# Second layer of a convolution + feed-forward kernel: a fourth product by a second level of Strassen, one unit fewer, and the jobs around it moved

## The chip, the cores and the metric

The kernel runs on one core of one Trainium2 chip. A core has five engines, each with its own in-order queue: TensorE (PE in the profile; its weight loads are PEld), VectorE (DVE), ScalarE (ACT), GpSimd (POOL) and SyncE (SP, which here only issues DMAs). They meet by semaphores. SBUF is the on-chip memory, PSUM the memory that TensorE writes (eight banks of 128 x 512 floats, used here as four slots of two banks). Transfers run on 16 DMA engines that all queues share; GpSimd's queue is q0 in the profile, SyncE's q1. The metric is the device time of one execution in microseconds.

## What is computed

```python
# x: (8, 4096, 192), weight: (8 heads, 7), w_in: (192, 2048), w_out: (2048, 192)
w = softmax(weight, axis=-1)                      # 7 taps per head
y[b, s, c] = sum_k w[c // 24, k] * x_pad[b, s + k, c]     # causal, 6 zeros ahead
h = y.reshape(32768, 192) @ w_in
g = h * np.clip(h + 3.0, 0.0, 6.0) / 6.0
out = g @ w_out                                   # (32768, 192)
```

All in float32.

## The kernel before

The tokens go in 32 blocks of 1024, each as two groups of 512 (the token halves). Block 0 runs by a plain path at start-up (`out_direct`, L379). Blocks 1 to 31 run `first_layer` (L498) and then `second_layer` (L586), and while one block is in these, VectorE and ScalarE prepare y of the next one.

**Convolution.** `conv_jobs` (L990) makes seven jobs: one ScalarE multiplication (L992) and six VectorE taps (L994) that each read x and y and write y (128 x 1536). They are hung into the stream of the other work by hand: `jobs` of the first layer (L1047: after step n of 16) and `between` of the second (L1058, L1060: at a unit of its clock). y is split into a high part (ScalarE, L476), a low one (VectorE, L1011) and a mixed one (L479), so that the first layer can run in TensorE's fast float32r form; `swap_parts` (L492) then issues six DMAs from GpSimd's queue that copy the three parts with their partition halves exchanged into `y_other`. `y_other` lies in the same memory as `z2` of the second layer.

**First layer.** 16 steps n. Each is 18 matmuls in three groups of six: HIGH and LOW (`begin`, L517), then MIX (`end`, L530). Between them the PSUM result is scaled (L522 on ScalarE; for n = 15 one half on ScalarE, L525, and one on VectorE, L526). After MIX come `relu` on ScalarE (L302) and the gate on VectorE (L306), which writes g and frees the step's PSUM slot; with four slots, step n + 2 begins in the slot of step n - 2. Steps 0 to 7 use y's own parts, steps 8 to 15 `y_other`. In TensorE's order a first layer has 48 groups of six; the last five are HIGH and LOW of n = 15 and MIX of n = 13, 14 and 15.

**Sums for the second layer.** g has four quarters A11, A21, A12, A22 (`g4`, L274): half of the 2048 hidden units by token half. The second layer multiplies them with w_out by Strassen's seven products P1 to P7 (`prod`, L417), of sums such as S1 = A21 + A22 (made in A21's place by DMAs with addition, L556), S2 = S1 - A11 (L414, `g_sums`), S3 = A11 - A21 (L414, in `s3`) and S4 = A12 - S2 (made in `s3` by L678 on ScalarE and adding DMAs, L679). Each product has three column groups q of 32. For P1, P2 and P5 the groups 0 and 1 are computed by Strassen once more, on halves of tokens and of the hidden units; this needs four smaller sums each (`small_sums`, L564; line L575): P1's by GpSimd during the first layer, in pairs of slots, into `shared`; P2's by VectorE into `z2`; P5's by VectorE into A22's place. Their weight sums `w_s` are made once (`small_weights`, L577).

**Second layer.** TensorE runs four streams side by side, each 32 columns wide, which write different partition quarters. The streams' order is written out by hand: `plain` (L621) is eight matmuls of 512 tokens at two units each, or some of them; `small` (L637) is one small product of four matmuls of 256 tokens at one unit each. All matmuls have one line, L616. `put` counts each stream's clock; `do(t, job)` hangs a job of another engine in at unit t; at the end all are sorted by unit and emitted in that order (L846), so each engine's queue has the order of these numbers. A product in plain form costs 16 units a column group, so 32 for two; by Strassen it costs 28. Before, all streams end at unit 81. Partial results are handed on inside PSUM by small ScalarE copies (L613, L750 to L755); `fold` (L673) adds up a second-level product on VectorE; the results are added (L458), transposed (L464) and stored by SyncE (L374), 128 bytes to a packet. `finish` (L801) does the last two of a block's four stores at the start of the next first layer.

PSUM slots: the second layer's banks `d, e, b, x_, a, c` (L589) lie in the slots of steps 12, 13 and 14, in this order by twos, and `f, h` in that of step 15. S1, as GpSimd's queue has it in the first layer: the pairs' sums for P1 (after n = 1, 3, 5, 7), then S3's first pair (after n = 9), a DMA into S1, S3's second pair (after n = 11), its DMA, and two more DMAs behind S3's last pairs, which VectorE makes (after n = 13 and 15).

Of the kernel before, what the change touches and what calls it, by code (L numbers as in the profile page):

```python
# [8 lines left out]
ALU = mybir.AluOpType  # L9
# [16 lines left out]
def kernel(  # L26
# [93 lines left out]
    w_s = cst.tile([P, 3, 4, NP // 2, QS], F32, name="w_s")  # L120
# [240 lines left out]
    def new_results():  # L361
        results[:] = [shared]
        xts[:] = 4, 5, 7
# [126 lines left out]
    y_own, y_other, pools = [], [None], []  # L490

    def swap_parts(dma=nc.sync):  # L492
        y_other[0] = pools[0].tile([P, 3, K3, N], F32, name="y_other", tag="other")
        for n in range(3):
            swap(y_other[0][:, n], y_own[n], dma)


    def first_layer(i, jobs):  # L498
# [44 lines left out]
        for n in range(count):  # L543
            if n == count - 3:
                begin(n + 2)
            end(n)
            if n < count - 3:
                begin(n + 2)
            for job in jobs.get(n, ()):
                job()  # L550
            if n < NP and n % 2:
                small_sums(shared, A11, (1, 2, 3, 4), nc.gpsimd, every[n - 1 : n + 1])
            if n > NP and n % 2:
                pair = slice(n - NP - 1, n - NP + 1)
                g_sums(nc.gpsimd if n + 3 < count else nc.vector, (3,), range(NP)[pair], 2)
                nc.gpsimd.dma_start(out=S1[:, pair], in_=A22[:, pair], accum_op=ALU.add)  # L556
# [20 lines left out]
    def small_weights(to, w):  # L577

        b11, b12, b21, b22 = (
            w_out[:, c::2, w, q * QS : (q + 1) * QS] for c in range(2) for q in range(2)  # L580
        )
        t1, t2, t3, t4 = (to[:, n] for n in range(4))
        for o, p, q in ((t1, b12, b11), (t2, b22, t1), (t3, b22, b12), (t4, b21, t2)):
            nc.gpsimd.tensor_tensor(out=o, in0=p, in1=q, op=ALU.subtract)

    def second_layer(i, between):  # L586
        last = i + 1 == NB
        ours = [free_slots.pop(0) for _ in range(3)]
        d, e, b, x_, a, c = (psum[:, 2 * n + k] for n in ours for k in range(2))  # L589
        z = pools[0].tile([P, NP + 1, N], F32, name="z2", tag="other")  # L590
# [10 lines left out]
        A, E, B, C = (bank[fourth, t] for bank in (e, x_) for t in halves)  # L601
        A2, E2, C2, B2 = f[first, lo], f[second, hi], h[first, lo], h[second, hi]
# [34 lines left out]
        def small(n, m_, out, start=False, j=3):  # L637
# [3 lines left out]
                1: (shared, w_s[:, 0]), 5: (s5, w_s[:, 1]), 2: (sums2, w_s[:, 2]),  # L641
            }[n]
            x11, x12, x21, x22 = four_parts(x)
            z1, z2, z3, z4 = four_parts(sums)
            b11, b12, b21, b22 = (
                w_out[:, h::2, w, q * QS : (q + 1) * QS] for h in range(2) for q in range(2)
            )
            t1, t2, t3, t4 = (ws[:, k] for k in range(4))
# [44 lines left out]

        plain(0, d, 4, 0, every, True)
        small(2, 1, A2, True, 0)
        after(0, copy, out=B2, in_=A2)
        plain(0, c, 7, 0, every[:3], True)
        by_half(0, a, 2, 2, 2, 1)
        after(0, copy, out=a[fourth], in_=a[first])
        plain(0, c, 7, 0, every[3:])  # L700
        small(2, 7, C2, False, 0)
        after(0, lambda: copy(out=p2(second, hi), in_=C2))
        small(2, 2, A2, False, 0)
        after(0, lambda: copy(out=p2(first, lo), in_=A2))
        plain(0, b, 6, 0, every)
        small(2, 4, C2, False, 0)
        p3(0)

        plain(1, d, 4, 1, every, True)
        plain(1, a, 2, 2, every[:2], True)  # L710
        by_half(1, a, 2, 2, 2, 0)
        after(1, copy, out=a[first], in_=a[second])
        plain(1, c, 7, 1, every[:2], True)
        small(2, 6, B2, False, 1)
        after(1, copy, out=C2, in_=B2)
        plain(1, c, 7, 1, every[2:])
        small(2, 5, E2, True, 1)
        after(1, lambda: copy(out=p2(second, lo), in_=E2))
        plain(1, b, 6, 1, every)
        small(2, 3, B2, False, 1)  # L720
        p3(1)

        plain(2, d, 4, 2, every[:6], True)
        plain(2, b, 1, 2, every[2:])
        after(2, copy, out=p1[third], in_=b[third])
        plain(2, c, 7, 2, every, True)
        plain(2, d, 4, 2, every[6:])
        by_half(2, a, 2, 2, 5, 1)
        plain(2, b, 6, 2, every)
        plain(2, a, 2, 2, every[6:])  # L730
        p3(2)

        def level_two(n, p, chunks, order):
            chunks, first_fill = list(chunks), [True]
            left = [list(chunks) for _ in halves]

            def fill_half(t, k):
                for _ in range(k):
                    ch = left[t].pop(0)
                    x, w = prod[n]  # L740
                    put(3, 1, lambda ch=ch: matmul(
                        3, (a, c)[t][fourth, halves[t]], w_out[:, ch, w, 2 * QS : 3 * QS],
                        x[:, ch, halves[t]], ch == 0,
                    ))

            def fill(k):
                plain(3, b, n, 2, [chunks.pop(0) for _ in range(k)], first_fill.pop() if first_fill else False)

# [6 lines left out]
                3: lambda: (copy(out=p()[first, hi], in_=C), fold(p(), B)),  # L755
            }
            to = {1: A, 2: A, 6: B, 5: E, 7: C, 3: B, 4: C}
            for step in order.split():
                if step[0] == "x":
                    fill(int(step[1]))  # L760
                elif step[0] in "lh":
                    fill_half("lh".index(step[0]), int(step[1]))
                else:
                    k = int(step)
                    small(n, k, to[k], k in (1, 5))
                    if k != 4:
                        do(clock[3], steps[k])

        level_two(1, lambda: p1, (), "1")
        plain(3, b, 1, 2, every[:2], True)  # L770
        after(3, copy, out=b[third], in_=V)
        level_two(1, lambda: p1, (), "6 2 7 5 4 3")
        plain(3, a, 2, 2, every[3:5])
        by_half(3, a, 2, 2, 5, 0)
        after(3, copy, out=a[third], in_=a[fourth])
        level_two(
            5, lambda: late["p5"], range(NP),
            "1 l8 6 2 7 5 4 3 h8" if last else "1 x6 6 2 7 5 4 3 x2",
        )
# [3 lines left out]
        do(0, small_sums, sums2, A12, (1, 2, 3, 4), nc.vector)  # L783
        do(33, tiles)
        do(28.5, g_sums, nc.vector, (2,), every[:4], 4)
        do(33, g_sums, nc.vector, (2,), every[4:], 4)
        do(35, copy, out=b[m], in_=p1)
        do(45, small_sums, s5, S1, (1, 2, 3, 4), nc.vector)
        for n, t in zip(range(0, NP, 2), (34, 39, 42, 45)):
            do(t, negative, slice(n, n + 2))  # L790
        do(41.2, lambda: copy(out=late["p7"], in_=c[m]))
        do(61.2, lambda: add(late["u3"], b[m], late["p7"]))
        do(62, lambda: add(late["p7"], late["u3"], d[m]))
        do(62, lambda: store(i, late["p7"], 1, 0))
# [79 lines left out]
    with tc.manual_schedule():  # L874
# [131 lines left out]
        def split_high():  # L1006
            high_of(y_own[HIGH][:], y[:])
# [87 lines left out]
```

## Time and profile before

| | |
|---|---|
| median of 3 runs (lowest, highest) | 2214.92 us (2214.84, 2214.95) |
| the profiled execution's own time | 2214.33 us |
| its span, first to last instruction | 2212.6 us |
| TensorE clock granted | 1.0 |
| busy: PE, PEld, DVE | 2205.5, 1619.9, 1888.4 us |
| busy: ACT, POOL | 1613.6, 1070.3 us |
| DMA: GpSimd's queue q0, SyncE's q1 | 47.8%, 14.6% of 16 engines' span |
| taps L994: 186, mean | 1.804 us |
| gates L306 of 128 x 1024: 496, mean | 1.218 us |
| GpSimd L414, 128 x 1024: 62, mean | 3.377 us |
| VectorE L575 of 128 x 1024: 124, mean | 1.222 us |
| adding DMA into S1 (512 KB), issue to landing | 5.7 us |
| swap of y (384 KB), issue to landing | 8.7 us |

The profile page gives the busy time of each engine, the chain of work that ended last (followed back from the last instruction), and the costliest groups: line, engine, operation, output <- input, shape and count, busy time and the mean of one, and the idle time of the engine ahead of them with whoever ended it. The timeline gives the same in order of time: start, length, engine and line, and in brackets the idle time before. All matmuls are pipelined, so that a busy PE need not be a PE at its peak, and a wait is put down to what came last. A share of busy time is an average over both layers; the stages have different limits.

### The profile page before, as it was taken

The page shows a single profiled execution, that of the slowest core. Times are in us where ns is not written, and L with a number is a line of the kernel's source. Part 1 is how long each engine was busy: PE and PEld are TensorE (multiplying, and loading weights), DVE is VectorE, ACT ScalarE, POOL GpSimd, SP SyncE. Part 2 cuts the span into 40 slices and gives each one's busy share as a digit, 9 for nine tenths or more (in the row PEclk, how much of TensorE's full clock was granted, in tenths as well). Part 3 has the DMA queues.
Part 4 walks back from the last instruction along what each step waited for, and adds up shares of the span by engine and source line. Part 5 has one row for each costly group of instructions (what it writes and reads, how often), then busy time and mean ns, then how long its engine had stood idle before and what let it go on. Part 6 is the DMA issues. An engine that isn't in the chain of part 4 may idle for free.

```text
span 2212.6 us, 53012 instructions
## 1 busy us (share of the span) xinstructions
PE 2205.5 (100%) x22364; PEld 1619.9 (73%) x22364; DVE 1888.4 (85%) x1766; ACT 1613.6 (73%) x2112; POOL 1070.3 (48%) x1029
## 2 busy tenths in 40 slices
PE   9999999999999999999999999999999999999999
PEld 5477777778777878777777777877777787777876
DVE  8888888888888888888888888888888888888876
ACT  7478776687766777767877668776677776687765
POOL 2455544455544555445554345554355544555533
PEclk9999999999999999999999999999999999999999
DMA  6265657656577656675565766666755667656575
GB/s 157 55 117 113 130 106 148 118 109 124 115 131 136 105 110 129 116 149 103 113 127 110 142 122 110 119 120 125 141 102 112 131 111 148 110 112 129 98 134 91
DMA packets 304190, 264.28 MB, mean 119 GB/s; under 512 B 210992, under 2 KB 216112, under 8 KB 303952
## 3 DMA queue, kind: packets, MB, share of 16 engines
q0 software_dynamic: 82240, 201.95, 47.8%
q1 hardware_dynamic: 220472, 58.67, 14.6%
q8 instruction: 175, 2.87, 0.6%
q14 instruction: 63, 0.52, 0.1%
q10 hardware_dynamic: 1240, 0.27, 0.1%
HBM read 31.72 MB, written 25.17 MB: 26 GB/s over the span
## 4 chain that ended last, share of the span: by engine, by line
PE 99%; DVE 0%; DMA 0%; SPq 0%; ACT 0%; issue 0%; DVEq 0%; ACTq 0%
PE psum L616 49%; PE psum L510 46%; PE psum L296 2%; PE psum L341 2%; DMA x<-in_x_dram 0%; DVE shared L458 0%; DVE shared L464 0%; SPq L100 0%; SPq L133 0%; DVE top L175 0%; PE psum L889 0%; DVE y L255 0%; SPq L89 0%; ACT y L903 0%; ACT scale L186 0%
## 5 line engine op out<-in xcount | busy, mean ns | idle before, releaser
L616 PE MATMUL psum<-g,w_out 128*32 128x512 f32 (+1 forms) x6340 | 899.5, 525 | 0.0
L306 DVE SCALAR_TENSOR_TENSOR g<-g,psum 128x1024 f32<-128x1024 f32 (+1 forms) x528 | 620.9, 1186 | 186.1 <-ACT g L302 185.7
L302 ACT ACTIVATE g<-psum,half 128x1024 f32<-128x1024 f32 (+1 forms) x528 | 564.9, 1087 | 6.0 <-PE psum L510 5.2
L616 PEld LDWEIGHTS psum<-g,w_out 128*32 128x32 f32 x6340 | 389.6, 110 | 217.6 <-issue 102.7
L510 PE MATMUL psum<-y,w_in 64*128 64x512 f32 x4464 | 522.2, 388 | 0.0
L510 PE MATMUL psum<-y_other,w_in 64*128 64x512 f32 x4464 | 516.6, 386 | 0.0
L522 ACT ACTIVATE psum<-psum 128x1024 f32<-128x1024 f32 x465 | 469.0, 1009 | 51.1 <-PE psum L510 48.8
L616 PE MATMUL psum<-s,w_out 128*32 128x512 f32 (+1 forms) x3024 | 503.7, 585 | 0.0
L510 PEld LDWEIGHTS psum<-y,w_in 64*128 64x128 f32 x4464 | 429.0, 184 | 100.8 <-issue 26.0
L510 PEld LDWEIGHTS psum<-y_other,w_in 64*128 64x128 f32 x4464 | 438.9, 184 | 67.0
L575 POOL TENSOR_TENSOR shared<-g 128x256 f32<-128x256 f32 x248 | 273.9, 1105 | 301.9 <-DVE g L306 301.9
L994 DVE SCALAR_TENSOR_TENSOR y<-x,c_sb,y 128x1536 f32<-128x1536 f32 x186 | 335.5, 1804 | 2.6 <-ACT y L992 1.4
L679 POOL DMA_DIRECT2D s<-g x124 | 148.5, 1202 | 341.1 <-ACT s L678 303.7
L616 PE MATMUL psum<-g,w_s 128*32 128x256 f32 x1488 | 285.5, 379 | 0.0
L556 POOL DMA_DIRECT2D g<-g x124 | 150.0, 1210 | 149.3 <-issue 76.8
L414 POOL TENSOR_TENSOR s<-g 128x1024 f32<-128x1024 f32 x62 | 209.4, 3377 | 24.8 <-DVE g L306 24.7
L616 PEld LDWEIGHTS psum<-s,w_out 128*32 128x32 f32 x3024 | 156.2, 110 | 53.3 <-issue 32.9
L616 PEld LDWEIGHTS psum<-g,w_s 128*32 128x32 f32 x1488 | 159.2, 110 | 42.6
L613 ACT COPY psum<-psum 32x512 f32<-32x512 f32 x186 | 89.4, 481 | 116.5 <-PE psum L616 113.4
L616 PE MATMUL psum<-shared,w_s 128*32 128x256 f32 x744 | 170.7, 379 | 0.0
L616 PE MATMUL psum<-z,w_s 128*32 128x256 f32 x744 | 170.6, 379 | 0.0
L575 DVE TENSOR_TENSOR g<-g 128x1024 f32<-128x1024 f32 x124 | 146.4, 1222 | 17.6 <-PE psum L616 14.4
(111 smaller groups left out, 2182.3 us busy)
## 6 DMA issues: line engine op xcount, KB each, us to landing
y_other<-y POOLq DMA_DIRECT2D x180, 384.0 KB, 8.7
g<-g POOLq DMA_DIRECT2D x124, 512.0 KB, 5.7
s<-g POOLq DMA_DIRECT2D x124, 512.0 KB, 6.6
out_dram<-shared SPq DMA_DIRECT2D x378, 64.0 KB, 4.0
x<-in_x_dram SPq DMA_DIRECT2D x53, 388.5 KB, 5.8
stage<-in_moe_w_in_dram SPq DMA_DIRECT2D x16, 192.0 KB, 4.4
stage<-in_moe_w_out_dram SPq DMA_DIRECT2D x8, 384.0 KB, 5.6
x<-in_x_dram SPq DMA_DIRECT2D x7, 384.0 KB, 4.6
```

The lines of the kernel that those rows point to most:

```text
L296: nc.tensor.matmul(out=psum[:, b], lhsT=w[r], rhs=src, start=start, stop=stop, skip_group_check=onto,)
L302: nc.scalar.activation(r6, h, ACT.Relu, bias=half[:], scale=1.0 / 6.0)
L306: nc.vector.scalar_tensor_tensor(out=g_, in0=g_, scalar=1.0, in1=h, op0=ALU.min, op1=ALU.mult)
L414: engine.tensor_tensor(out=o[:, r], in0=a[:, r], in1=b[:, r], op=op)
L510: nc.tensor.matmul(out=psum[:, 2 * slots[n] + k], lhsT=r32(w_in_parts[part][r, c, s]), rhs=r32(y_other[0][r, part, s] if group else y_own[ ...
L522: nc.scalar.mul(both(n), both(n), 4097.0)
L556: nc.gpsimd.dma_start(out=S1[:, pair], in_=A22[:, pair], accum_op=ALU.add)
L575: engine.tensor_tensor(out=o, in0=p, in1=q, op=op)
L613: streams[3].append((t - 0.5, lambda: fn(*args, **kw)))
L616: nc.tensor.matmul(out=out, lhsT=w, rhs=x, start=start, stop=True, tile_position=(0, j * QS), skip_group_check=True,)
L679: nc.gpsimd.dma_start(out=S3[:, pair], in_=A12[:, pair], accum_op=ALU.add)
L994: jobs.append(lambda k=k: nc.vector.scalar_tensor_tensor(out=y[:], in0=x[:, :, k : k + N], scalar=c_sb[:, k : k + 1], in1=y[:], op0=ALU.mu ...
```

## The change

- P4 = A22 x T4, columns 0 and 1, also by Strassen once more. Its four sums go into a new tile `z4`, which shares its memory with y's three own parts (pool `later`, tag `own`): GpSimd makes the first after n = 8 and the third after n = 9, VectorE the second after n = 14 and the fourth at the head of the second layer. Its results go to free places in `shared` (slots 4 and 5).
- The streams are written anew for 80 units: stream 0 begins with P4's third column group in bank b, stream 1 with P1's third column group in b, streams 2 and 3 with the first small products of P4 and P1. S1 times T1 (P5) is begun by stream 3 at unit 4. The bank letters `x_` and `a` change places.
- S3's third and fourth pair are both made after n = 15, by VectorE.
- y's parts come later in the second layer, since their memory holds `z4` before: high at 37, low at 62, mix at 63 (before: 9, 20, 46).
- One convolution tap a block is done as a multiplication on GpSimd into `s3` and an adding DMA onto y from GpSimd's queue, issued at the head of the next first layer, behind the six swaps; four taps follow on VectorE after n = 5, 7, 9 and 11, and one at unit 24 of the second layer. Before, VectorE did two taps at the end of the second layer, one at the head of the first and three after n = 1, 5 and 9.
- The weights' small sums are kept for four products; the third of each takes the place of a block of w_out that is no longer used.

The core of the diff:

```diff
-    w_s = cst.tile([P, 3, 4, NP // 2, QS], F32, name="w_s")
+    w_s = cst.tile([P, 4, 3, NP // 2, QS], F32, name="w_s")
...
-        xts[:] = 4, 5, 7
+        xts[:] = 7, 4, 5
...
-            if n > NP and n % 2:
-                pair = slice(n - NP - 1, n - NP + 1)
-                g_sums(nc.gpsimd if n + 3 < count else nc.vector, (3,), range(NP)[pair], 2)
-                nc.gpsimd.dma_start(out=S1[:, pair], in_=A22[:, pair], accum_op=ALU.add)
+            if n == NP:
+                sums4[:] = [pools[0].tile([P, NP, N], F32, name="z4", tag="own")]
+                small_sums(sums4[0], A22, (1,), nc.gpsimd)
+            if n in (NP + 1, NP + 3, count - 1):
+                for p in ((n - NP - 1) // 2,) if n < count - 1 else (2, 3):
+                    pair = slice(2 * p, 2 * p + 2)
+                    g_sums(nc.gpsimd if p < 2 else nc.vector, (3,), range(NP)[pair], 2)
+                    nc.gpsimd.dma_start(out=S1[:, pair], in_=A22[:, pair], accum_op=ALU.add)
+            if n == NP + 1:
+                small_sums(sums4[0], A22, (3,), nc.gpsimd)
+            if n == count - 2:
+                small_sums(sums4[0], A22, (2,), nc.vector)
...
-        d, e, b, x_, a, c = (psum[:, 2 * n + k] for n in ours for k in range(2))
+        d, e, b, a, x_, c = (psum[:, 2 * n + k] for n in ours for k in range(2))
...
-        plain(0, d, 4, 0, every, True)
+        plain(0, b, 4, 2, every, True)
         small(2, 1, A2, True, 0)
...
-        plain(1, d, 4, 1, every, True)
...
+        plain(1, b, 1, 2, every, True)
...
-        plain(2, d, 4, 2, every[:6], True)
...
+        level_two(4, lambda: p4, (1,), 2)
+        plain(2, c, 7, 2, every[:2], True)
+        level_two(4, lambda: p4, rest, 2)
+        plain(2, c, 7, 2, every[2:])
...
+        level_two(1, lambda: p1, (1,))
+        fill_half(0, 4) if last else fill(2)
+        level_two(1, lambda: p1, rest)
+        level_two(5, lambda: late["p5"], (1,))
+        plain(3, a, 2, 2, every[2:6])
+        fill_half(0, 4) if last else fill(4)
+        level_two(5, lambda: late["p5"], rest)
+        fill_half(1, 8) if last else fill(2)
+        assert clock == [80] * 4
...
-        do(0, small_sums, sums2, A12, (1, 2, 3, 4), nc.vector)
-        do(33, tiles)
+        do(0, small_sums, sums2, A12, (1, 2), nc.vector)
+        do(0, small_sums, sums4[0], A22, (4,), nc.vector)
+        do(0, small_sums, sums2, A12, (3,), nc.vector)
         do(28.5, g_sums, nc.vector, (2,), every[:4], 4)
+        do(32, tiles)
+        do(32, fold_with, p1)
         do(33, g_sums, nc.vector, (2,), every[4:], 4)
...
-        do(45, small_sums, s5, S1, (1, 2, 3, 4), nc.vector)
+        do(36, small_sums, s5, S1, (1, 2, 3, 4), nc.vector)
+        do(37, small_sums, sums2, A12, (4,), nc.vector)
+        do(38, fold_with, p4, 2)
...
+        def tap_by_dma(x, k):
+            to = S3[:, 0:K3]
+            nc.gpsimd.tensor_scalar(
+                out=to, in0=x[:, :, k : k + N], scalar1=c_sb[:, k : k + 1], scalar2=None,
+                op0=ALU.mult,
+            )
+            nc.gpsimd.dma_start(out=y[:], in_=to, accum_op=ALU.add)
...
-            jobs = {4 * n + 1: [job] for n, job in enumerate(conv[4:])}
-            jobs[-1] = left + conv[3:4]
+            jobs = {3 + 2 * n: [tap] for n, tap in enumerate(taps[:5]) if n}
+            k = KC - len(taps)
+            jobs[-1] = [lambda: tap_by_dma(conv_x[0], k)] * bool(taps) + left
...
-                between = [(9, split_high), (20, split_low), (46, split_mix), (70, lambda: swap_parts(nc.gpsimd))]
+                between += [(37, split_high), (62, split_low), (63, split_mix)]
+                between += [
+                    (t, lambda n=n: swap_parts(nc.gpsimd, (n,)))
+                    for n, t in ((HIGH, 70), (LOW, 70), (MIX, 70))
+                ]
...
-                between += [(20, begin_conv), (60, lambda: conv[0]()), (72, lambda: conv[1]()), (73, lambda: conv[2]())]
+                between += [(30, begin_conv), (74, lambda: conv[0]())]
```

## The prediction, made before the changed kernel had run

> **What bounds the kernel now.** I read the page first, then the chain that ended last, then one block on each engine in the timeline (block 14: first layer from 983.41 to 1016.32 us, second layer to 1051.36), then the DMA issues. The page gives TensorE the whole span, and so does the chain:
>
> ```profile
> span 2212.6 us, 53012 instructions
> PE 2205.5 (100%) x22364; PEld 1619.9 (73%) x22364; DVE 1888.4 (85%) x1766; ACT 1613.6 (73%) x2112; POOL 1070.3 (48%) x1029
> PE 99%; DVE 0%; DMA 0%; SPq 0%; ACT 0%; issue 0%; DVEq 0%; ACTq 0%
> ```
>
> The chain in order of time is a strict alternation, 32.9 us of first layer and 35.04 us of second layer:
>
> ```profile
> 847.54 32.95 PE psum L510 x286
> 880.49 35.04 PE psum L616 x256
> 915.53 32.91 PE psum L510 x288
> 948.44 35.04 PE psum L616 x255
> ```
>
> The same numbers come back for all 31 blocks, and inside a first layer six matmuls always take 0.68 us. So TensorE never waits: whatever it saves counts in full, and whatever it is made to wait counts in full. In the second layer one unit is 0.43 us (matmuls of one stream start 0.43 apart; 81 units are 34.8 of the 35.04).
>
> VectorE around the end of the first layer (start, length, line, idle before and who ended it):
>
> ```profile
> 1008.07 1.81 DVE L994 SCALAR_TENSOR_TENSOR y<-x,c_sb,y 128x1536 f32<-128x1536 f32 x1
> 1009.80 2.44 DVE L306 SCALAR_TENSOR_TENSOR g<-g,psum 128x1024 f32<-128x1024 f32 x2
> 1013.05 1.22 DVE L306 SCALAR_TENSOR_TENSOR g<-g,psum 128x1024 f32<-128x1024 f32 x1 [0.81 <-ACT g L302]
> 1014.41 0.70 DVE L526 TENSOR_SCALAR psum<-psum 128x512 f32<-128x512 f32 x1
> 1016.28 1.22 DVE L306 SCALAR_TENSOR_TENSOR g<-g,psum 128x1024 f32<-128x1024 f32 x1 [1.16 <-ACT g L302]
> ```
>
> The gate that starts at 1016.28 is that of n = 13. It waits for its relu, which waits for TensorE, so it ends at 1017.50 and cannot end earlier: 1.18 us after TensorE entered the second layer. GpSimd in the same first layer:
>
> ```profile
> 1000.08 2.25 POOL L575 TENSOR_TENSOR shared<-g 128x256 f32<-128x256 f32 x1 [0.74 <-DVE g L306]
> 1002.40 0.74 POOL L575 TENSOR_TENSOR shared<-shared,g 128x256 f32<-128x256 f32 x1
> ...
> 1008.23 3.92 POOL L414 TENSOR_TENSOR s<-g 128x1024 f32<-128x1024 f32 x1 [0.79 <-DVE g L306]
> 1012.46 1.24 POOL L556 DMA_DIRECT2D g<-g  x1 [0.30 <-POOL s L414]
> ```
>
> One 128x256 sum takes 0.74 us beside gates (which read PSUM) but 2.25 beside a convolution tap (L994, two SBUF inputs, 999.91 to 1001.72): it ends 0.61 after the tap. The 3.92 ends 2.27 after the tap that began at 1008.07. So the two do not overlap. Start-up shows the other direction: a tap that begins while GpSimd works takes 2.01 instead of 1.81, and ends 1.62 after GpSimd's op (102.78).
>
> ```profile
> 102.39 2.01 DVE L994 SCALAR_TENSOR_TENSOR y<-x,c_sb,y 128x1536 f32<-128x1536 f32 x1
> 101.72 1.06 POOL L584 TENSOR_TENSOR w_s<-w_out,w_s 128x128 f32<-128x128 f32 x1
> ```
>
> **The change, part by part**, against the profiled execution's own 2214.33 us (the median of the runs is 2214.92, 0.6 more).
>
> *One unit less.* P4's columns 0 and 1 cost 28 units instead of 32, over four streams: 81 to 80. Gain 0.43 us a block, 31 blocks: 13.3 us.
>
> *P4 comes first, in bank b.* The built program's first second-layer matmul now waits for gate 13, since b lies in that gate's PSUM slot. Before, stream 3 asked for this gate at unit 4 (1.72 us in, when it was done) and bank d needed only gate 12. Price: 1017.50 − 1016.32 = 1.2 us in every block. Nothing hides it, TensorE's queue is in order. It alone is 37 us, more than the gain.
>
> *P5 starts at unit 4.* Stream 3 now fills with P5 (S1) at unit 4; the program waits there for the first adding DMA into S1, and stream 2 beside it for the first pair of S3. Before, S1 was first asked for at unit 37, 15.9 us in; the DMA (issued 1012.46, landing 5.1 to 6.0 later) was done by then by far. This decides the forecast, so I lay out GpSimd's queue. It gets, ahead of S3's first pair (its 128x1024 difference), another 128x1024 sum (z4's first). The taps move to n = 5, 7, 9, 11. With the rule "one at a time, by turns" from the rows above:
> - Tap 5 at 999.91 as now; the four sums of the third pair, begun beside it, end at 1004.53 as now.
> - Gate 7 ends 1004.07 (its relu sets that). Tap 7 begins at 1003.99, is held to 1004.53 and ends 1.62 later: 1006.15.
> - The last pair's sums need gate 7 and are held to 1006.15; the first ends 0.6 later, three more by 0.70: 1008.9.
> - Gates 8 and 9 end 1008.4; tap 9 is held to 1008.9, ends 1010.5. z4's sum is held to that and takes 2.28: 1012.8.
> - Gates 10 and 11 end 1012.8; tap 11 ends 1014.45. S3's first pair: 1016.75.
> - 0.3 to the DMA's issue, 5.3 to its landing (rows 5.1 to 6.0): 1022.35.
>
> TensorE would reach unit 4 at 1016.32 + 1.72 = 1018.04: it waits 4.3 us, call it 4.4 with the wake-up. The 1.2 for gate 13 lies inside that.
>
> By the Trainium skill ("SBUF — State Buffer", section "Who interferes with whom") a VectorE instruction with two SBUF inputs and a GpSimd instruction that reads SBUF exclude each other for a whole instruction, the second blocking fully. The trace agrees in both directions (2.25 against 0.74, 2.01 against 1.81). Without that rule the layout above would have no holds: last sums 1006.9, z4 1009.2, S3 1011.5, DMA landed 1017.1, and only the 1.2 would be left (2238 us).
>
> *VectorE's order.* The upper half's scaling (L526) now follows tap 11 and gate 12: 1014.4 + 1.15 + 0.7 = 1016.3 against 1015.1, while TensorE wants it at 1015.54: 0.7 us. Inside the 4.4, as both only move TensorE's place. VectorE's second sum of z4 (needed at unit 8) and S3's last pairs come later than now, held once by GpSimd's second 2.28; with TensorE 4.4 later they are in time. Per block VectorE gets two 1.22 sums and a fold (0.85) and loses a tap (1.8): its 58.5 busy of this block (26.75 and 31.74 in its two stretches) becomes 60, plus some 3 of holds, of a block of 72.
>
> *S1's other pairs.* They are now needed at units 33 to 35 (37 to 40 before). Layout: z4's other GpSimd sum goes first, 1017.85 to 1020.1; VectorE's sum for z4, held by it, ends 1021.2; the second difference ends 2.28 later, 1023.5. Then 0.3 to the issue, 1.7 to the first packet (1.6 to 1.85 for the three of this block that find the queue empty), three DMAs at 2.8 each (four take 11.5 us on the queue from 1034 on), 0.2: landed 1034.1. Unit 35 is at 1020.7 + 15.0 = 1035.7: in time by 1.6 us. Were TensorE not held at unit 4, it would be held here; so this price replaces, it does not add.
>
> *The tap by GpSimd and DMA.* The trace has no such GpSimd op. Bounds: half of a two-input sum of this size (1.7) and one whole (2.28 x 1.5 = 3.4); I take 3.4. GpSimd idles from the swaps (0.5 each) to 991.97, so either costs nothing. The adding DMA moves 768 KB: 4.2 us at the 2.8 us per 512 KB above. But the swaps of y now wait for later VectorE work: splits of low and mix, fold and sum stand before the sum that frees y_other's buffer, so the first issue is 0.6 us before the next first layer (3.7 before it now); the six swaps hold the queue for 11 to 12.6 us. The tap's DMA lands 14.8 to 16.6 us into the first layer; VectorE's first tap is due at 16.5. I take no wait; the other end is a rival.
>
> *Nothing:* more ScalarE copies (nine of 0.35 a block; ScalarE is busy 19.4 of the 35.04 us of that stage); four more 128x128 sums at start-up, under GpSimd's idle 3 us before 108.36; the end, unchanged.
>
> Sum: 2214.3 − 13.3 + 30 x 4.4 + 1.2 (the last block has no taps, so only gate 13 counts) = 2334.4, as a median of runs **2335 us**.
>
> **The rivals.**
> - *Only gate 13 counts*, or S3 and its DMA come nearly in time (holds shorter than laid out): stalls of 1.2 to 3.0 us a block. For it: gates never hold GpSimd. Against: 2.25 and 3.92 beside every tap. 2238 to 2293.
> - *The adding DMA is late.* The output stores (128-byte packets) share the engines with it, or it moves slower than 2.8 us per 512 KB. VectorE's queue stops at tap 5, gates 6 and on stand behind it, TensorE waits for their PSUM slots and all the above moves with it. It decides from 17 us into the layer on; 1 to 3 us late: 2365 to 2425.
> - *Faster.* TensorE's wait at the head of the second layer is absorbed: the records' modelled ends make TensorE seem further ahead of gate 13 than it is, and stalls stay under 0.43 us a block. Place: the first matmul of P4; price zero, 2201 us. Against: the wait is in the program, and VectorE's 1.16 of idle before this gate names ScalarE, not VectorE's load.
> - *It doesn't do what it says:* the built program has 3384 wide and 3536 narrow second-layer matmuls instead of 3818 and 2792: exactly one unit less a block. Ruled out.
>
> **How the numbers follow.** Forecast (3.0 to 5.5 us of stall) 0.52; only gate 13 or little more 0.24; late DMA 0.14; faster 0.08; within 0.2% (about what a measurement of this kernel can tell from no change) 0.02. So slower 0.90. The range leaves out the faster case, no change and the upper half of the late DMA (0.17): 2238 to 2390.
>
> **What would show it.** In the changed kernel: a TensorE gap after the first layer ended by VectorE's gate; a second one four units later, ended by the S1 DMA or GpSimd's difference; GpSimd sums of over 2 us beside three taps; VectorE taps of over 2 us; second layers of 38 us or more between first layers of 33 to 34. I am wrong if the second layer stays near 34.6, or if TensorE waits mainly inside the first layer, behind tap 5.

## The result, and the profile after

The changed kernel takes **2398.66 us** (median of four runs, 2391.43 to 2401.39) against 2214.93 before: 1.0825 times as long, 95% interval 1.0800 to 1.0849. Slower, as forecast, but 64 us more than the 2335 predicted and 9 us above the range.

The head of the profile page of the changed kernel (span; busy time by engine; the chain that ended last, by engine), with the tap group of VectorE and the new adding DMA (KB, median us from issue to landing):

```profile
span 2389.6 us, 55082 instructions
PE 2271.1 (95%) x22984; PEld 1479.5 (62%) x22984; DVE 2019.1 (84%) x1891; ACT 1694.2 (71%) x2329; POOL 1364.8 (57%) x1155
PE 51%; DMA 16%; DVE 12%; POOL 10%; issue 7%; ACT 3%; SPq 1%; DVEq 0%; POOLq 0%; ACTq 0%
L1032 DVE SCALAR_TENSOR_TENSOR y<-x,c_sb,y 128x1536 f32<-128x1536 f32 x156 | 351.7, 2255 | 46.4 <-DMA y<-s 44.2
y<-s POOLq DMA_DIRECT2D x30, 768.0 KB, 11.0
```

TensorE was 99% of the chain before; now it is half, and most of the rest is what it waits for. The chain in order of time shows one block (start, length, what):

```profile
904.85 6.90 PE psum L635 x40
911.74 1.61 PE psum L511 x10
...
915.19 4.20 POOL s L1021
...
919.68 10.06 DMA y<-s
...
929.77 1.82 DVE y L1032
931.59 1.14 DVE g L306
...
932.77 12.18 PE psum L511 x102
...
947.35 0.10 DVE psum L527
...
949.17 14.25 PE psum L635 x144
...
964.76 0.35 ACT psum L632
...
965.15 17.46 PE psum L635 x112
```

It reads as three stalls, none of them at unit 4: the first layer (L511) waits for tap 5 (L1032), which waits for the adding DMA; then it waits for VectorE's upper scaling (L527); the second layer (L635) waits half way for a ScalarE copy (L632). The waits of TensorE's matmuls in all (us, times, longest; ends of matmuls are modelled, so these are a little under the distances between starts that I use below):

```profile
PE psum L511 <- DVE psum L527: 51.4, 23, 2.2
PE psum L511 <- DVE g L306: 33.0, 31, 2.7
PE psum L635 <- DMA g<-g: 12.6, 6, 2.9
```

The lengths below run from the first matmul of a layer to the first of the next; a stall is the time between two matmul records beyond their usual distance. Spans differ by 2389.6 − 2212.6 = 177.0 us:

| | us |
|---|---|
| 31 first layers, mean 37.17 against 32.92 | **+131.6** |
| – last MIX matmuls, waiting for the upper scaling, 23 blocks x 2.6 | 60.2 |
| – begin of step 10 (gate 6 behind tap 5 behind the DMA), 30 blocks | 36.6 |
| – border to the second layer (gate 13), 21.6 against 9.8 | 11.8 |
| – half clock (below) | 4.0 |
| – the rest: shorter gaps, not followed up one by one | 19 |
| 30 second layers, mean 36.35 against 35.04 | **+39.1** |
| – one unit less | −12.9 |
| – half clock | 23.3 |
| – what undisturbed layers (35.06) take above 35.04 less one unit, 30 x 0.45; 0.30 of it is the copy at unit 36 (e4) | 13.5 |
| – other waits, 14.4 of it in 5 blocks, from unit 4 on | 15.2 |
| last second layer and start; 1.7 of it half clock, 2.9 a wait for the transfer into S1 | +6.3 |

**The turn at tap 11.** Timeline of the same block (start, length, idle before in brackets):

```profile
938.36 3.91 POOL L584 TENSOR_TENSOR z<-g 128x1024 f32<-128x1024 f32 x1
942.20 4.05 DVE L1032 SCALAR_TENSOR_TENSOR y<-x,c_sb,y 128x1536 f32<-128x1536 f32 x1
942.24 2.40 POOL L414 TENSOR_TENSOR s<-g 128x1024 f32<-128x1024 f32 x1
946.17 1.21 DVE L306 SCALAR_TENSOR_TENSOR g<-g,psum 128x1024 f32<-128x1024 f32 x1
947.30 0.69 DVE L527 TENSOR_SCALAR psum<-psum 128x512 f32<-128x512 f32 x1
948.04 0.97 PE L511 MATMUL psum<-y_other,w_in 64*128 64x512 f32 x5 [2.21 <-DVE psum L527]
```

When z4's sum ends, tap 11 and GpSimd's subtraction stand side by side, 0.04 us apart. In 23 of the 30 blocks GpSimd gets the turn: 2.40 for it, 4.05 for the tap, and the gate and the scaling behind the tap are late. In 5 the tap gets it, as in this block, whose second layer begins at 1092.03: the subtraction takes 4.02, S1 is late, and TensorE waits at unit 4, as the forecast had it:

```profile
1086.81 1.81 DVE L1032 SCALAR_TENSOR_TENSOR y<-x,c_sb,y 128x1536 f32<-128x1536 f32 x1
1086.86 4.02 POOL L414 TENSOR_TENSOR s<-g 128x1024 f32<-128x1024 f32 x1
1097.63 1.08 PE L635 MATMUL psum<-g,w_out 128*32 128x512 f32 x3 [2.82 <-DMA g<-g]
```

In the last 2 the adding DMA lands so late that tap 11 begins only after the subtraction; there TensorE's long wait is at step 10 (2.3 and 2.9 us). Less the half clock, a block of the first kind takes 72.5 us, of the second 73.6, of the third 72.8: the turn decides where TensorE waits, hardly how long. The start times do not tell the first kind from the second (the tap's is 0.03 to 0.05 us ahead in both), so what gives the turn is not shown.

**The clock.** Stretches of the changed kernel (bounds, length, busy time of PE, PEld, DVE, ACT, POOL, then the granted clock, DMA share, GB/s):

```profile
872.31:875.72 3.41, 1.77 (x17) 1.01 (x21) 3.41 (x4) 1.49 (x2) 3.41 (x2) 1.00 0.89 154
875.72:879.13 3.41, 3.41 (x26) 1.27 (x20) 3.41 (x4) 0.87 (x3) 2.10 (x2) 0.50 0.18 32
943.99:947.40 3.41, 1.84 (x17) 1.18 (x13) 3.41 (x3) 2.70 (x3) 3.11 (x3) 1.00 0.22 38
947.40:950.81 3.41, 2.62 (x29) 1.49 (x33) 3.41 (x4) 1.12 (x1) 3.41 (x2) 1.00 0.68 116
```

Seventeen times within the work the clock is 0.50 for exactly 3.413 us, and all these stretches lie on one grid of 3.413 us. Each costs 1.7 us (a second layer with one takes 36.76, an undisturbed one 35.06), 29 in all. Before the change there is none.

### The profile page after: what moved, and what is told of

Its sections match the earlier page's. It is cut to its first block, busy times and chain, and to the rows that moved or that the text cites. A ratio compares the mean times of both kernels' runs of the same rounds, so it can differ in the third digit from the quotient of the medians.

```text
span 2389.6 us, 55082 instructions
## 1 busy us (share of the span) xinstructions
PE 2271.1 (95%) x22984; PEld 1479.5 (62%) x22984; DVE 2019.1 (84%) x1891; ACT 1694.2 (71%) x2329; POOL 1364.8 (57%) x1155
## 3 DMA queue, kind: packets, MB, share of 16 engines
q1 hardware_dynamic: 220472, 58.67, 13.5%
## 4 chain that ended last, share of the span: by engine, by line
PE 51%; DMA 16%; DVE 12%; POOL 10%; issue 7%; ACT 3%; SPq 1%; DVEq 0%; POOLq 0%; ACTq 0%
PE psum L635 41%; DMA y<-s 11%; PE psum L511 7%; DVE g L306 6%; DVE y L1032 5%; POOL s L1021 4%; DMA out_dram<-shared 3%; PE psum L296 2%; PE psum L341 2%; POOL y_other L267 2%; POOL y_other L266 1%; ACT psum L632 1%; POOL shared L584 1%; DMA g<-g 1%; ACT g L302 1%
## 5 line engine op out<-in xcount | busy, mean ns | idle before, releaser
L635 PE MATMUL psum<-g,w_out 128*32 128x512 f32 (+1 forms) x5968 | 904.3, 520 | 21.9 <-DMA g<-g 12.6
L635 PE MATMUL psum<-s,w_out 128*32 128x512 f32 (+1 forms) x3024 | 676.0, 587 | 1.2 <-DMA s<-g 1.2
L511 PE MATMUL psum<-y_other,w_in 64*128 64x512 f32 x4464 | 552.2, 393 | 84.5 <-DVE psum L527 51.4
L511 PEld LDWEIGHTS psum<-y_other,w_in 64*128 64x128 f32 x4464 | 422.7, 185 | 203.0 <-DVE psum L527 64.0
L635 PEld LDWEIGHTS psum<-g,w_out 128*32 128x32 f32 x5968 | 355.3, 113 | 297.1 <-issue 126.5
L511 PE MATMUL psum<-y_own,w_in 64*128 64x512 f32 x4464 | 521.9, 388 | 0.0
L511 PEld LDWEIGHTS psum<-y_own,w_in 64*128 64x128 f32 x4464 | 424.2, 184 | 105.4 <-issue 26.0
L1032 DVE SCALAR_TENSOR_TENSOR y<-x,c_sb,y 128x1536 f32<-128x1536 f32 x156 | 351.7, 2255 | 46.4 <-DMA y<-s 44.2
L584 POOL TENSOR_TENSOR shared<-g 128x256 f32<-128x256 f32 x248 | 230.3, 929 | 103.0 <-DVE g L306 103.0
L635 PE MATMUL psum<-g,w_s 128*32 128x256 f32 x1488 | 283.5, 380 | 0.0
L635 PEld LDWEIGHTS psum<-s,w_out 128*32 128x32 f32 x3024 | 187.8, 110 | 85.8 <-issue 24.9
L635 PE MATMUL psum<-z,w_out 128*32 128x256 f32 x992 | 235.1, 380 | 2.4
L635 PE MATMUL psum<-z,w_s 128*32 128x256 f32 x992 | 237.0, 383 | 0.3 <-DVE z L584 0.2
L584 POOL TENSOR_TENSOR z<-g 128x1024 f32<-128x1024 f32 x62 | 205.3, 3311 | 0.0
L266 POOL DMA_DIRECT2D y_other<-y_own x90 | 48.8, 542 | 265.3 <-issue 246.6
L414 POOL TENSOR_TENSOR s<-g 128x1024 f32<-128x1024 f32 x62 | 163.6, 2639 | 0.0
L414 DVE TENSOR_TENSOR g<-g 128x2048 f32<-128x2048 f32 x62 | 142.0, 2290 | 19.9 <-issue 18.9
```

Of the source, the lines that this page charges most:

```text
L266: dma.dma_start(out=to[D2:P], in_=part[0:D2])
L414: engine.tensor_tensor(out=o[:, r], in0=a[:, r], in1=b[:, r], op=op)
L511: nc.tensor.matmul(out=psum[:, 2 * slots[n] + k], lhsT=r32(w_in_parts[part][r, c, s]), rhs=r32(y_other[0][r, part, s] if group else y_own[ ...
L584: engine.tensor_tensor(out=o, in0=p, in1=q, op=op)
L635: nc.tensor.matmul(out=out, lhsT=w, rhs=x, start=start, stop=True, tile_position=(0, j * QS), skip_group_check=True,)
L1032: jobs.append(lambda k=k: nc.vector.scalar_tensor_tensor(out=y[:], in0=x[:, :, k : k + N], scalar=c_sb[:, k : k + 1], in1=y[:], op0=ALU.mu ...
```

## The experiments

Theory: the losses have separate causes, of which the largest is the turn between VectorE and GpSimd at tap 11. Rival, the recorded one: GpSimd's chain into S1 has its own date, and TensorE waits for that wherever the other waits are taken away. Summary (first and second layers: means; border: sum of the distances between the last matmul of a first layer and the next; MIX: sum and number of the stalls of over 1 us ahead of the last MIX; half clock: stretches; all times in us; one profile each):

| | time | ratio to before, 95% | first | second | border | MIX (times) | half clock |
|---|---|---|---|---|---|---|---|
| before | 2214.9 | | 32.92 | 35.04 | 9.8 | 0 | 0 |
| changed | 2398.7 | 1.0800–1.0849 | 37.17 | 36.35 | 21.6 | 60.2 (23) | 17 |
| e1 tap 11 | 2364.9 | 1.0665–1.0697 | 36.24 | 36.60 | 48.3 | 0 | 4 |
| e2 VectorE tap | 2352.0 | 1.0600–1.0661 | 36.01 | 36.70 | 21.7 | 60.4 (23) | 17 |
| e3 banks | 2388.1 | 1.0764–1.0800 | 36.95 | 37.26 | 10.9 | 55.1 (21) | 24 |
| e4 copy | 2382.9 | 1.0739–1.0771 | 37.10 | 36.30 | 22.6 | 55.0 (21) | 17 |
| e5 e1 to e4 | 2322.1 | 1.0472–1.0504 | 33.36 | 37.97 | 9.8 | 0 | 1 |
| e6 no subtraction | 2314.0 | 1.0419–1.0487 | 35.77 | 35.09 | 33.7 | 0 | 1 |
| e7 P2 first | 2340.9 | 1.0556–1.0592 | 33.36 | 38.75 | 9.8 | 0 | 0 |
| e8 sums on VectorE | 2313.5 | 1.0433–1.0468 | 33.35 | 37.82 | 9.8 | 0 | 0 |
| e9 late DMA | 2285.3 | 1.0307–1.0338 | 34.58 | 35.62 | 9.8 | 0 | 0 |
| e10 taps moved | 2277.3 | 1.0272–1.0303 | 33.68 | 36.26 | 9.8 | 0 | 0 |
| e11 taps left out | 2226.1 | 1.0040–1.0074 | 32.95 | 35.30 | 9.8 | 0 | 0 |

**e1: tap 11 into the second layer.**

```
-            jobs = {3 + 2 * n: [tap] for n, tap in enumerate(taps[:5]) if n}
+            jobs = {3 + 2 * n: [tap] for n, tap in enumerate(taps[:4]) if n}
-            now = taps[5:]
+            now = taps[4:]
```

> Edit: the VectorE tap behind step 11 goes into the second layer (unit 24, beside the tap that is there). Theory A (the tap itself is what makes VectorE's upper scaling late): the 2.6 us stall ahead of the last MIX matmuls goes (60.2 us in the changed kernel's profile), and the 17 half-clock stretches, which all follow it or another long stall, go with it (some 29 us): 2310 to 2340 us. Theory B (GpSimd's subtraction and its adding DMA into S1 are late by as much, as the prediction had it): S1 lands no earlier, so TensorE now waits some 2 us at unit 4 of the second layer instead, and the time is 2365 to 2395 us. I take B for the likelier.

2364.9 us: at the lower end of B by the total, but not by its place. The MIX stall is gone, and with it 13 half-clock stretches. What comes in its stead is gate 13 at the border (48.3 in place of 21.6) and some 0.6 near unit 8 in 20 blocks; at unit 4 TensorE arrives as the transfer lands.

**e2: the DMA tap back on VectorE.**

```
-            jobs[-1] = [lambda: tap_by_dma(conv_x[0], k)] * bool(taps) + left
+            jobs[-1] = left + taps[:1]
```

> Edit: the tap that GpSimd computes and an adding DMA puts into y is done by VectorE at the first layer's begin instead. Theory A (only the landing costs): the wait behind tap 5 (group 29, 36.6 us) goes and the stall ahead of the last MIX (60.2 us) stays: about 2355 to 2365 us. Theory B (GpSimd's 4.2 us also push its later sums, and so its subtraction onto VectorE's last tap): the MIX stall goes in most blocks too: 2290 to 2330 us. Rival to both: VectorE's extra 1.8 to 2.2 us at the begin delay gates 0 to 3 and TensorE waits there: over 2380 us.

2352.0, 47 us less, close under A's figure: the wait at step 10 is gone, and the MIX stall stays, in 23 blocks as before. In the other 7 the tap gets the turn (1.81), and TensorE waits 2.2 us on average at unit 4. So GpSimd's 4.2 us are not what brings its subtraction onto tap 11; only the landing costs.

**e3: other banks.**

```
-        d, e, b, a, x_, c = (psum[:, 2 * n + k] for n in ours for k in range(2))
+        b, e, a, d, x_, c = (psum[:, 2 * n + k] for n in ours for k in range(2))
-            2: [bank[third, t] for bank in (a, d) for t in halves],
+            2: [bank[third, t] for bank in (e, d) for t in halves],
-        free_slots.extend(ours[n] for n in (0, 2, 1))
+        free_slots.extend(ours[n] for n in (1, 2, 0))
```

> Edit: the banks of the second layer are dealt out anew, so that the first matmul of each stream goes into the two banks of step 12 (P4's small chain takes the rows of e that were free), not of step 13. Theory: the idle time between the layers (21.6 us in all) falls to the 10 us of the kernel before, so 12 us less, and a stall that straddles the border loses 0.3 us in its clock window, so some of the 17 half-clock stretches go too (1.7 us each): 2365 to 2387 us. Rival (another wait, for gate 14 or S1, takes the place): 2395 to 2400 us.

The border falls by 10.7 us as expected. The gain in time is 10.6, just outside the forecast, and not much clear of the scatter: the runs span 2384.1 to 2413.9, those of the changed kernel 2391.4 to 2401.4. The half-clock stretches did not get fewer in the profiled execution, which is the slowest of the five (24 stretches, granted clock 0.982); in the fastest the clock is 0.988.

**e4: one copy earlier.**

```
-        do(32.2, copy, out=D2, in_=B2)
+        do(28.1, copy, out=D2, in_=B2)
```

> Edit: one of ScalarE's copies between PSUM rows (the seed of the M3 chain) is made right behind the copy at unit 28 instead of behind a 0.55 us copy at unit 32. The changed kernel's undisturbed second layers take 35.06 us though they have one unit less than the 35.04 us of before; TensorE stands 0.5 us in every one of them at unit 36, where its wait ends with this copy. Theory: 30 times 0.45 us, 13 us less, with undisturbed second layers of 34.6 us: 2383 to 2388 us. Rival (the columns' own pace sets it, or the next copy in ScalarE's queue is as late): second layers stay at 35.06 and the time at 2396 to 2400 us.

2382.9, 15.8 us less, and the weight loads' wait for L632 falls from 18.1 to 4.0 us. The shortest second layers come to 34.76, not 34.6: the copy had cost 0.30 of the 0.43 us that the 81st unit took, 9 us over 30 blocks. The two profiled executions differ by no more than 5.4 us, so the rest of the 15.8 is not shown to be the copy's.

**e5: the four together.**

> Edit: the four edits of e1 to e4 together. Theory A (the waits are separate, so the gains add): 12 to 16 us for the copy, 11 for the banks, 34 for the late tap, 47 for the tap by DMA: about 2290 to 2300 us. Theory B (the transfer into S1 has its own date: GpSimd's subtraction ends some 33.6 us after the first layer's begin, as in e1, and its transfer 4.6 us later, whatever TensorE does): TensorE now gets to unit 4 some 35 us after the begin and waits 3 to 3.5 us there, and each such wait empties more than 1.9 us of one clock window, so 1.7 us for a half-clock stretch come on top: 2201 + 30 x 5 = about 2350 us, with the waits at unit 4 and none in the first layer. Theory C (nothing else is late): 2200 to 2220 us.

2322.1: above A (2290 to 2300), below B (2350). The border is that of before and the first layers are nearly so, but the second layers are 3 us longer. Timeline of e5's second layer, which begins at 916.78:

```profile
915.53 1.24 POOL L561 DMA_DIRECT2D g<-g  x1 [0.30 <-POOL s L414]
918.65 2.84 POOL L414 TENSOR_TENSOR s<-g 128x1024 f32<-128x1024 f32 x1
919.02 3.57 DVE L584 TENSOR_TENSOR z<-z,g 128x1024 f32<-128x1024 f32 x1
920.61 0.12 PEld L635 LDWEIGHTS psum<-g,w_out 128*32 128x32 f32 x3 [1.25 <-DMA g<-g]
922.73 0.38 PE L635 MATMUL psum<-z,w_s 128*32 128x256 f32 x1 [0.20 <-DVE z L584]
```

Here is the recorded forecast's wait: at unit 4 (918.5) for the transfer into S1, which was issued at 915.53; and right behind it one for P4's own sum (z), 3.57 us on VectorE beside GpSimd's subtraction. B's place is right; its price is less, as the waits come in smaller pieces and only one half-clock stretch is left (in the last block).

**e6: GpSimd's first subtraction left out** (in the changed kernel).

```
-                    g_sums(nc.gpsimd if p < 2 else nc.vector, (3,), range(NP)[pair], 2)
+                    if p:
+                        g_sums(nc.gpsimd if p < 2 else nc.vector, (3,), range(NP)[pair], 2)
```

> Leaves out: GpSimd's first subtraction into S3 (P7's first two chunks are then computed from other data); its adding DMA stays. All else is the changed kernel. Theory (the shared lock: VectorE's last tap takes 4.05 us because this subtraction runs from 0.04 us after the tap was issued): the tap takes 1.8 to 2.3 us and the 2.6 us stall ahead of the last MIX falls under 1 us in most blocks; the transfer into S1 also goes out 2.4 us sooner, so no new wait at unit 4: 2310 to 2350 us. Rival (the tap is slow for its own reasons, its operands or the traffic of the transfers): still 4 us a tap, 2385 to 2400 us.

2314.0, the median of two runs that lie 13 us apart. Its timeline at the same place:

```profile
905.26 3.91 POOL L585 TENSOR_TENSOR z<-g 128x1024 f32<-128x1024 f32 x1
909.09 1.80 DVE L1033 SCALAR_TENSOR_TENSOR y<-x,c_sb,y 128x1536 f32<-128x1536 f32 x1
909.11 1.23 POOL L562 DMA_DIRECT2D g<-g  x1
911.95 0.69 DVE L527 TENSOR_SCALAR psum<-psum 128x512 f32<-128x512 f32 x1
```

Nothing stands beside the tap now and it takes 1.80; of the MIX stall 0.4 us a block is left. A subtraction of 2.4 us a block costs 85 us in all, by the means of the profiles about half of it in the first layers (37.17 to 35.77) and half in the second (36.35 to 35.09, without their half-clock stretches and waits at unit 4). The tap's operands are the same as before, and the transfer into S1 is now issued right beside it, so neither is the cause.

**e7: P2 instead of P5 at unit 4.** e5 and:

```
...
-        fill_half(0, 4) if last else fill(2)
+        plain(3, a, 2, 2, every[2:4], True)
+        do(clock[3], copy, out=a[second], in_=a[fourth])
...
-        plain(3, a, 2, 2, every[2:6])
-        fill_half(0, 4) if last else fill(4)
+        plain(3, a, 2, 2, every[4:6])
+        fill_half(0, 8) if last else fill(6)
...
```

> Edit: e5_all, and at units 4 to 7 stream 3 no longer fills with two chunks of P5 (S1, by the adding DMA) but with two chunks of P2 (A12, written by the gates); P5's come at unit 40. One more ScalarE copy a block. Theory B of e5: the wait at unit 4 goes, and TensorE waits only at unit 32 if at all: 2205 to 2240 us. Rival (the next thing behind the same engines, P4's sums at unit 8 or 16, takes its place): 2260 to 2340 us. If e5_all shows theory A or C, e7 is within 10 us of it.

The rival, and slower than e5: the stalls at unit 4 are gone; TensorE waits 1.9 us in all 30 blocks at unit 8 for P4's sum, and 0.9 at unit 40 for a ScalarE copy. Behind the wait for S1 stood the next one.

**e8: P4's two GpSimd sums on VectorE.** e5 and:

```
-                small_sums(sums4[0], A22, (1,), nc.gpsimd)
-            if n == NP + 1:
-                small_sums(sums4[0], A22, (3,), nc.gpsimd)
...
+                small_sums(sums4[0], A22, (1,), nc.vector)
...
+            if n == count - 1:
+                small_sums(sums4[0], A22, (3,), nc.vector)
```

> Edit: e5_all, and the two of P4's sums that GpSimd computes in the first layer (3.9 and 2.9 us there) are computed by VectorE instead, one between its upper scaling and gate 13, one behind gate 15. Theory A (the shared lock): VectorE's own sum takes 1.2 us instead of 3.6, GpSimd's subtraction and its transfer come 3 us sooner, the waits at units 4 and 8 go; VectorE pays 2.4 us for the two and gets 2.4 us back: second layers of 35.5 to 36.5 us, 2240 to 2275 us. Theory B (VectorE has no idle time left in e5's second layers, so only its sum of work counts, and that is unchanged): 2310 to 2330 us.

2313.5: theory B. The held sum and its wait are gone; TensorE waits 0.8 to 1.2 us at unit 4 for gate 14 instead, which stands behind the moved sum, and the second layers stay at 37.8. In e5's second layer VectorE is busy 37.05 of 37.75 us (third row; columns as above; the first row is a second layer of the kernel before):

```profile
880.49:915.53 35.04, 35.04 (x414) 22.78 (x414) 31.70 (x29) 19.36 (x34) 11.54 (x13) 1.00 0.77 133
883.43:916.78 33.35, 33.31 (x292) 26.94 (x289) 27.25 (x25) 30.80 (x32) 24.79 (x26) 1.00 0.45 90
916.78:954.53 37.75, 37.20 (x435) 21.21 (x433) 37.05 (x34) 22.00 (x41) 13.36 (x10) 1.00 0.79 139
```

Before, VectorE had 31.70 of 35.04 in this stage. In e8 it is busy 37.1 of 37.8 on the mean of 30 second layers. So VectorE has become the bound there; e11 below tests it.

**e9: the DMA tap late.** e8 without e1's and e2's edits; the product goes into free chunks of S3, the DMA behind step 7, VectorE's taps ahead of it:

```
...
+            jobs = {2 * n - 1: [tap] for n, tap in enumerate(taps[1:5]) if n}
+            jobs[7] = [add_product] * bool(taps)
+            jobs[-1] = [lambda: tap_product(conv_x[0], k)] * bool(taps) + left + taps[1:2]
```

> Edit: e8_vz, but one tap is GpSimd's again: its product is made at the first layer's begin into chunks of S3 that are free, and added to y by DMA behind step 7, after VectorE's taps (at the begin and behind steps 1, 3 and 5), so that none of them waits for it; one tap is left in the second layer. VectorE has 1.8 us a block less than in e8 and none of its taps is near GpSimd's late work. If VectorE's sum of work is what is left (theory B of e8): 1.8 x 30 = 54 us under e8, to 2205 at the least. Rival (the 4.2 us product puts GpSimd's sums behind VectorE's early taps, so gates 0 to 5 come late and TensorE stands in the first layer, or S1 is late again): within 20 us of e8 or above it.

2285.3, 28 us under e8, half of the forecast. The second layers fall to 35.6, but the first rise to 34.6, since the first tap meets the product:

```profile
874.65 4.19 POOL L1021 TENSOR_SCALAR s<-x,c_sb 128x1536 f32<-128x1536 f32 x1
874.90 4.68 DVE L1034 SCALAR_TENSOR_TENSOR y<-x,c_sb,y 128x1536 f32<-128x1536 f32 x1
```

**e10: that tap behind step 1**, the others behind 3, 5 and 7, the DMA behind 9; bank c into the slot of step 13.

```
+            jobs = {2 * n - 1: [tap] for n, tap in enumerate(taps[:5]) if n}
+            jobs[9] = [add_product] * bool(taps)
-        b, e, a, d, x_, c = ...
+        b, e, c, d, a, x_ = ...
```

> Edit: e9 with its first VectorE tap (4.7 us, of which 2.8 behind GpSimd's product) moved from the first layer's begin to behind step 1, the others to steps 3, 5 and 7, the adding DMA to step 9; and bank c of the second layer in the slot of step 13, so that the matmul at unit 4 does not wait for gate 14. Theory (VectorE's time held by GpSimd is what delays the gates): the 1 us stall at group 11 goes and first layers come to 33.0 to 33.5 us, second layers to 35.0 to 35.3: 2225 to 2250 us. Rival (the tap behind step 1 delays gates 2 to 5 by as much as the held one did, since VectorE has no more than 0.8 us between gates): 2270 to 2290 us.

2277.3, the rival's figure. First layers fall by 0.9 us, second layers rise by 0.6: what VectorE does not finish in one stage it owes in the next. It is busy 35.13 of the 35.79 us of a second layer.

**e11: e10 with VectorE's taps left out** (all but the ScalarE step and GpSimd's, from the third block on).

```
-            k = KC - len(taps)
+            k = 1
...
-            taps = conv[1:]
+            taps = conv[1:2]
```

> Leaves out five of the six later convolution steps in each block from the third (all that VectorE does; the ScalarE step and GpSimd's stay). All else is e10. Theory (VectorE's sum of work is what is left between e10 and the pace of the matmuls): with 9 us a block taken off VectorE, first layers at 32.9 us and second layers at 34.6 us: 2200 to 2212 us, so the 80 units are then worth their 13 us. Rival (the new order of the 80 units itself costs something, waits on ScalarE's copies or GpSimd's transfers): 2215 to 2235 us.

2226.1: the rival again. With 9 us a block taken off VectorE the first layers are those of before (32.95), but the second layers take 35.3, the shortest 34.9, not 34.6; the weight loads wait 104 us for "issue", nothing that the profile names. So some 51 us of e10 are VectorE's load. Even without it this order gains nothing over 81 units: the kernel before took 2213.7 beside these runs. Why the 80 units run 0.3 us above their pace is not settled. A version that beats the kernel before did not come out of this.

## Why the prediction was wrong

The direction and its cause held. What failed is the path: the forecast put nearly the whole price at unit 4 of the second layer, 30 x 4.4 = 132 us, and put the adding DMA, the copies and the clock at nothing. By its own sign ("if TensorE waits mainly inside the first layer, behind tap 5") it was wrong: 131.6 of the 177.0 us lie in the first layers, though only 36.6 of them behind tap 5. That the total still came within 9 us of the range is in part luck: the stalls that stand in place of the 132 come to 106, by another path, and hide part of what was left out.

- *Slower, by TensorE waiting for VectorE and GpSimd:* this was right.
- *Layout of GpSimd's queue:* the step that failed is "tap 11 ends 1014.45. S3's first pair: 1016.75". It gave the turn to the tap. GpSimd had it in 23 of 30 blocks; without its subtraction, or with the tap elsewhere, the stall ahead of the last MIX goes (e6, e1). GpSimd's own date was right: its subtraction ends 33.0 us after the first layer's begin (944.64 − 911.67), forecast 33.3. So its transfer is in time, and what the forecast had at unit 4 of the second layer stands ahead of the last MIX, 2.6 us instead of 4.4, with the rest of the 4.4 at tap 5 and gate 13. I priced the scaling's delay at 0.7, "Inside the 4.4"; it became the main stall.
- *Trainium skill, SBUF ("SBUF — State Buffer", section "Who interferes with whom"):* the exclusion itself is confirmed (4.05, 4.68 and 3.57 against 1.81 and 1.21 alone). The section's "Issue order, not op shape, decides who blocks" gave no forecast of the turn: by the records the tap was 0.03 to 0.05 us ahead in every block where the two met, and lost in 23 and won in 5.
- *The adding DMA, "I take no wait":* this was wrong, and the rival named for it had the mechanism. In this block the product starts 3.5 us into the layer, takes 4.19 (3.4 assumed), and the transfer takes 10.1 from issue to landing, so it lands 18.1 us into the layer, not 14.8 to 16.6. It cost 36.6 us in stalls; taking it away gained 47 (e2).
- *"Nothing: more ScalarE copies":* this was wrong. One copy behind a 0.55 us one made TensorE wait at unit 36 of every block; it cost 0.30 us a block, 9 of the unit's 13.3 us. Another 0.15 a block keeps undisturbed layers above their count and is not settled (e4).
- *Gate 13, 1.2 us a block, inside the rest:* this was right. Where no other stall precedes it, the border is 1.56 in place of 0.31 (e1, 48.3 in all), and with other banks the wait goes (e3, e5).
- *The clock:* the forecast has no term for it. It cost 29 us, near half of the 64 by which the forecast was short. The rest of the 64: 36.6 and 13.5 more, for the DMA and for what undisturbed second layers take too much; 4 for the last block and the unit; 7, by which the median lies above the profiled execution; against some 26 less in the stalls that the 4.4 stood for (60.2 + 11.8 + 19 + 15.2 = 106.2 against 132). The recorded sum itself comes to 2334.2, not 2334.4.
- *VectorE has room ("60, plus some 3 of holds, of a block of 72"):* true only of a block of 72. At the 67.5 the change aims at (32.92 + 34.61), VectorE is the bound of the second layer (e5, e8, e10; e11 without its taps).

## What to carry to other kernels

A layer that saves matmul time by more sums has to be paid on VectorE and GpSimd in the same stage: count what these engines do per stage, held time included, against the stage's length as it should become. Where two instructions that exclude each other become ready together, price both orders, for the loser is late either way and whatever stands behind it in its queue with it. Repairing waits one at a time shows the next wait, not the gain: e5 took 77 us away at once and then stood at VectorE's load.

## What was not expected of the hardware

TensorE's granted clock falls to half for a window of 3.413 us when the window before, on a fixed grid, had too much idle time. I counted as idle what lies between matmul records beyond one matmul's length. Seven profiles have such stretches (changed, e1 to e6; 81 within the work). Every one followed a window with 1.90 us of idle or more, and no window with over 1.97 was without one. In the rows above, 872.31 has 1.90 of it and is followed by 0.50, 943.99 has 1.72 and is not. The page's busy column, whose ends are modelled, separates them less sharply. So a stall costs 1.7 us more when it fills over some 55% of a window: 2.6 us stalls did so or not by how they lay on the grid, and the same stall time in pieces (e5: 1 stretch, e7 and e8: none) did not.

Of the 81 stretches 74 last one window and 7 (six in e2, one in e3) last two, as here in e2 (columns as above):

```profile
644.59:648.00 3.41, 3.10 (x17) 1.59 (x21) 3.41 (x4) 1.11 (x1) 3.16 (x2) 0.50 0.60 103
648.00:651.42 3.42, 3.42 (x24) 1.16 (x20) 3.42 (x4) 0.69 (x2) 1.23 (x2) 0.50 0.52 91
651.42:654.83 3.41, 3.41 (x48) 1.64 (x44) 3.38 (x4) 0.45 (x2) 2.40 (x2) 1.00 0.92 157
```

In these 7 the first half-clock window had 0.52 to 0.61 us of idle (a matmul counted twice as long there); in the other 74 it had 0.41 at most. So a short wait in a window that is already at half clock kept the clock there for another one.

The Trainium skill ("TensorE: Matmul & The Clock Gate", section "Part 1: The HAM clock gate (the "warmup" mystery)") has the free-running window of 3413 ns and the half clock "after ≥1 idle window"; the grid and the length agree, but here a window was enough in which TensorE was idle for little over half.
